# Hash logits in two packed products per half, and scores ahead of the transposes in every third step

## The chip, the cores and the metric

The kernel runs on one core of a Trainium2 chip. The metric is the device time of the whole program in microseconds. The engines are TensorE (PE in the rows; its weight loads are PEld), VectorE (DVE), ScalarE (ACT), GpSimd (POOL) and SyncE, whose queue (SPq) issues most transfers.

## What is computed

LSH attention over 16 heads (batch 2, 8 heads) of 768 tokens and 64 dimensions, all in float32, and then two dense layers with 1536 tokens:

```
q_bits = (q @ proj > 0); k_bits = (k @ proj > 0)         # proj: 64 x 6
mask   = (bucket(q_bits)[:, None] == bucket(k_bits)[None, :])
scores = where(mask, q @ k.T / sqrt(64), -1e9)
attn   = exp(scores - max); attn /= sum(attn) + 1e-9
x      = attn @ v, as 1536 x 512
x      = gelu_sigmoid(x @ w_in) @ w_out                   # 512 -> 2048 -> 512
out    = mish(x @ w_in2) @ w_out2
```

The products must keep float32 precision, so the kernel splits each operand into a high part that TensorE takes at full speed (fp32r) and a rest, and adds three products: high by high, high by rest, rest by high.

## The kernel before

**Stages.** The attention fills the first 225 us. It is one loop over 96 steps (`NSTEP`); a step is a tile of 128 queries of one head, six steps (`NT`) a head. The two dense layers follow; their weights are fetched, decoded and split during the last heads already (`wfetch`, `wgo`), and so are sums of blocks of the first layer's weights (`ssums`, `ssplit`) and factors of the attention's result (`x_ops`), which the dense layers need.

**Scores with the mask in them.** `qk` (L613) makes a step's scores with four products of 384 columns: `kh` and `qx` carry the high part of k against q and its rest, `kb` and `qb` carry the rest of k and, in rows 0 to 63, the hash bits. These bits add a large number to every pair whose buckets differ, and `clamp` (L625, VectorE) cuts the score at 1e9 while it takes the row's minimum. `expo` (L638, ScalarE) is the exponential with the row sum.

**Transposes and values.** Three steps are a group. `trp` (L676) transposes the exponentials of three steps, three 128 x 128 blocks into one PSUM bank, of which there are three (`ps_t`, "pt"; the logits and the row sums use the same three). ScalarE casts a bank to the high part (`pth`, L683), VectorE subtracts it (`trl`, `ptl`, L688), and `pv` (L700, L701) multiplies both with v (`vv`). The transposes lag `LAG` = 3 steps behind the scores, the products with v 4.

**A head's preparation.** `prep(n)` gives the parts of head n; `start_prep` places them by step (`at(step, f)`, run where `T` stands in the order), counted from `b0` = 6 (n - 2), two heads ahead of the head's use, so in the same row of six steps as the attention of head n - 2. `load_q` and `load_k` bring 64 and 128 rows. On GpSimd `s0` and `s1` (at b0 + 2) scale q into its high part `qk_m` (L473), scale again and subtract for the rest (L476, L477 into `qx`), round k (`kh`, L109), and subtract (L481). A DMA copies the q part to the other partitions of `qx` (L474). At b0 + 8 `s2` makes the **logits**: `logits` (L493) is called for both halves of 384 tokens, and multiplies `qk_m`, `kh` and `qx` with a projection padded to 128 columns (`pwt`), six products into one bank, rows 64 to 127 for the first half and 0 to 63 for the second. In the same step VectorE compares and scales all 128 rows at once (`s2m`, constants in `mc`), and at b0 + 9 `s5` sends the mask's rows to `qb` and `kb` with four DMAs of 32 rows. `s4` sends two rests, `s3` makes `vv`.

**Row sums and result.** `norm1` to `norm3` transpose the row sums of two heads (L657), write them to DRAM and broadcast them (`rb`); `x_out` (L725, L731, L732) multiplies the result by them on GpSimd, and `x_split` and `x_ops` (L109, L301, L309, L313) make the factors.

**Order.** Within a step the string `ORDER` sets what each engine's queue gets: A and B the transposes, a and b the residues, C the clamp, E the exponential, Q the next step's scores, T the work placed by `at`, P and R the products with v. Every engine takes its instructions in this program order. `SSP` and `WOF` are tables of steps for the weight sums and for the first weights:

```
ORDER = "ACaBbETQPR"
SSP = (-13, -11, -10, -9, -7, -6)
```

Of the kernel before, what the change touches and what calls it, by code (L numbers as in the profile page):

```python
# [30 lines left out]
def mask_consts():  # L31
    c = np.zeros((64, 2), np.float32)
    c[12:18, 0] = -3.0e38
    c[0:18, 1] = 1.0
    c[38:44, 0] = -3.0e38
    c[32:38, 1] = -2.0 * CBIG
    c[38:50, 1] = CBIG
    return np.concatenate([c, c])
# [3 lines left out]
def lsh_attention_moe_kernel(  # L42
# [9 lines left out]
    nc = tc.nc  # L52
    B, H, D, S = qt.shape
    NTOK, DM = out.shape
# [11 lines left out]
    SSP = (-13, -11, -10, -9, -7, -6)  # L66
    WOF = ((-1, -1, 11, 14, 18), (-1, 1, 11, 13, 17))
# [3 lines left out]
    POOLW = ()  # L71
    X0 = (1, 6)
# [150 lines left out]
    def wsplit(k, sub):  # L223
# [127 lines left out]
    def attention():  # L351
        with ExitStack() as es:
# [79 lines left out]
            def zero_rows():  # L432
                for t in (kb_tiles[1], qb_tiles[1]):
                    pcopy(t[32:64], zero[32:64])

# [8 lines left out]
            def pcol(j, o):  # L444
                w = pw[:, j, o : o + 2 * NB * (2 if o else 1)]
                return w.rearrange("p (a b) -> p a b", a=2)[:, :, 0:NB]

            def prep_w():
# [6 lines left out]
                nc.scalar.mul(pcol(0, 0), rnd(pr), -1.0)  # L455

            opnd = {}

            def prep(n):
# [12 lines left out]
                def s0():  # L472
                    nc.gpsimd.tensor_scalar(qk_m[0:D], qn[0:D], QSCALE, 1.0, ALU.mult, ALU.mult)  # L473
                    nc.sync.dma_start(rnd(qx[D:P]), rnd(qk_m[0:D]))  # L474
                    if n > 1:
                        nc.gpsimd.tensor_scalar(qn[0:D], qn[0:D], QSCALE, 1.0, ALU.mult, ALU.mult)  # L476
                        nc.gpsimd.tensor_sub(qx[0:D], qn[0:D], rnd(qk_m[0:D]))  # L477

                def s1():
                    pcopy(kh, kn)  # L480
# [20 lines left out]
                def s2():  # L501
                    pt = ps_t.tile([P, 512], F32, tag="pt", name="prep")
                    logits(pt, 0, 64, True, False)
                    logits(pt, 1, 0, False, True)
                    mk_box.append(pt)
                    if n > 1:
                        s2m()

                def s2m():
                    pt = mk_box.pop()  # L510
# [6 lines left out]
                def s4():  # L517
                    nc.sync.dma_start(rnd(qb[D:P]), rnd(qk_m[0:D]))
                    nc.sync.dma_start(rnd(kb[D:P]), rnd(qk_m[D:P]))

                def s5():
                    mk = mk_box.pop()
                    for f in range(2):
                        c = slice(f * HS, (f + 1) * HS)
                        rows = (qb, f * D), (kb, f * D + 32)
                        for t, r in rows[::-1] if f else rows:
                            nc.sync.dma_start(rnd(t[0:32, c]), mk[r : r + 32])
# [62 lines left out]
                return s0, s1, s2, s3, s4, s5  # L590
# [162 lines left out]
            ORDER = "ACaBbETQPR"  # L753
            NZ = 5
            NZL = 2
            PVLAG = LAG + 1
            todo = {}

# [7 lines left out]
            at(1, zero_rows)  # L766

# [3 lines left out]
            def start_prep(n):  # L771
                b0 = NT * (n - 2)
                s0, s1, s2, s3, s4, s5 = prep(n)
# [17 lines left out]
            for u in range(NHD // 2):  # L791
# [6 lines left out]
                at(zs + nz + (2 if u < NHD // 2 - 1 else 1), norm3, u)  # L798
# [22 lines left out]
            for i in range(NSTEP + PVLAG):  # L821
# [14 lines left out]
                for op in ORDER if i != 2 else ORDER.replace("TQ", "QT"):  # L836
# [402 lines left out]
def layouts(q, k, v, proj, moe_w_in, moe_w_out, moe2_w_in, moe2_w_out):  # L1239
# [3 lines left out]
    qt = q.transpose(0, 1, 3, 2)  # L1243
# [44 lines left out]
```

## Time and profile before

| | before |
|---|---|
| median of three runs | 730.86 us (730.52 to 731.77) |
| the profiled execution | 731.06 us, of which its span is 729.3 us |
| mean granted TensorE clock | 0.999 |
| TensorE busy | 723.5 us, 99% |
| VectorE busy | 616.3 us, 85% |
| ScalarE busy | 469.0 us, 64% |
| GpSimd busy | 185.4 us, 25% |

The span runs from the first to the last instruction of one profiled execution; 1.8 us lie around it. Busy shares are means over the whole span. GpSimd's work lies nearly all in the attention, the first 225 us, so its share of that stage is much higher than 25%.

### The profile page before, as it was taken

The page shows a single profiled execution, that of the slowest core. Times are in us where ns is not written, and L with a number is a line of the kernel's source. Part 1 is how long each engine was busy: PE and PEld are TensorE (multiplying, and loading weights), DVE is VectorE, ACT ScalarE, POOL GpSimd, SP SyncE. Part 2 cuts the span into 40 slices and gives each one's busy share as a digit, 9 for nine tenths or more (in the row PEclk, how much of TensorE's full clock was granted, in tenths as well). Part 3 has the DMA queues.
Part 4 walks back from the last instruction along what each step waited for, and adds up shares of the span by engine and source line. Part 5 has one row for each costly group of instructions (what it writes and reads, how often), then busy time and mean ns, then how long its engine had stood idle before and what let it go on. Part 6 is the DMA issues. An engine that isn't in the chain of part 4 may idle for free.

```text
span 729.3 us, 11137 instructions
## 1 busy us (share of the span) xinstructions
PE 723.5 (99%) x3856; PEld 631.5 (87%) x3856; DVE 616.3 (85%) x1134; ACT 469.0 (64%) x957; POOL 185.4 (25%) x187
## 2 busy tenths in 40 slices
PE   8999999999999999999999999999999999999998
PEld 6999999999998788888888888888888888888886
DVE  8888889989888959878878797998699899897864
ACT  7888888888898765536546465576635656455340
POOL 7968877889893000000000000000000000000000
PEclk9999999999999999999999999999999999999999
DMA  5745656666624221121211221301302121211004
GB/s 157 199 125 145 190 141 163 182 157 153 170 85 118 109 70 48 58 87 64 82 58 58 88 88 60 112 0 59 115 0 87 59 75 69 88 58 58 1 1 173
DMA packets 25992, 69.53 MB, mean 95 GB/s; under 512 B 4464, under 2 KB 6992, under 8 KB 25936
## 3 DMA queue, kind: packets, MB, share of 16 engines
q1 hardware_dynamic: 25632, 68.62, 31.7%
q8 instruction: 30, 0.49, 0.3%
q10 hardware_dynamic: 304, 0.20, 0.1%
q14 instruction: 26, 0.21, 0.1%
HBM read 49.09 MB, written 3.19 MB: 72 GB/s over the span
## 4 chain that ended last, share of the span: by engine, by line
PE 94%; DVE 2%; ACT 2%; DMA 0%; issue 0%; DVEq 0%
PE y L947 36%; PE X L1010 11%; PE s L613 9%; PE pt L676 9%; PE Y L1010 8%; PE W L1010 7%; PE u L701 4%; PE u L700 4%; PE h L346 4%; PE prep L493 2%; ACT p L638 1%; DMA qn<-in_qt_dram 0%; ACT pth L683 0%; DVE gl L907 0%; DVE Y L1031 0%
## 5 line engine op out<-in xcount | busy, mean ns | idle before, releaser
L688 DVE TENSOR_TENSOR ptl<-pt,pth 128x384 fp32r<-128x384 f32 x192 | 98.1, 553 | 22.4 <-ACT pth L683 20.2
L683 ACT CAST pth<-pt 128x384 fp32r<-128x384 f32 x192 | 82.8, 484 | 28.7 <-PE pt L676 28.7
L638 ACT ACTIVATE p<-p,mn 128x768 f32<-128x768 f32 x96 | 91.2, 950 | 1.7 <-DVE p L625 1.6
L625 DVE TENSOR_SCALAR_CACHE_REDUCE p<-s 128x768 f32<-128x768 f32 x96 | 90.6, 945 | 0.3 <-PE s L613 0.2
L961 DVE TENSOR_TENSOR xq<-xq,y 128x512 f32<-128x512 f32 (+1 forms) x113 | 75.6, 679 | 13.7 <-PE y L947 13.0
L676 PE MATMUL pt<-ident,p 128*128 128x128 f32 x576 | 81.1, 274 | 0.1
L947 PE MATMUL y<-wh,gh 128*128 128x512 f32 (+1 forms) x194 | 75.4, 389 | 0.0
L947 PE MATMUL y<-wl,gh 128*128 128x512 f32 (+1 forms) x194 | 75.4, 389 | 0.0
L947 PE MATMUL y<-wh,gl 128*128 128x512 f32 (+1 forms) x194 | 75.2, 387 | 0.0
L947 PE MATMUL y<-gh,wh 128*128 128x512 f32 x192 | 75.0, 391 | 0.0
L947 PE MATMUL y<-gh,wl 128*128 128x512 f32 x192 | 74.9, 390 | 0.0
L947 PE MATMUL y<-gl,wh 128*128 128x512 f32 x192 | 74.7, 389 | 0.0
L259 ACT CAST wh<-wb 128x512 fp32r<-128x512 f32 x64 | 39.4, 620 | 54.5 <-DVE wb L246 26.2
L676 PEld LDWEIGHTS pt<-ident,p 128*128 128x128 f32 x576 | 68.5, 140 | 6.6 <-ACT p L638 2.4
L700 PE MATMUL u<-pth,vv 128*128 128x384 f32 x192 | 64.7, 337 | 0.0
L701 PE MATMUL u<-ptl,vv 128*128 128x384 f32 x192 | 64.5, 336 | 0.0
L613 PE MATMUL s<-kh,qx 128*128 128x384 f32 x192 | 55.7, 370 | 0.2 <-DVE p L625 0.2
L613 PE MATMUL s<-kb,qb 128*128 128x384 f32 x192 | 49.3, 337 | 0.3 <-POOL qk_m L473 0.2
L261 DVE TENSOR_TENSOR wl<-wb,wh 128x512 fp32r<-128x512 f32 x62 | 42.3, 687 | 3.9 <-ACT wh L259 3.6
L961 DVE TENSOR_TENSOR yr<-yr,y 128x512 f32<-128x512 f32 x56 | 38.2, 684 | 7.8 <-PE y L947 6.9
L947 PEld LDWEIGHTS y<-wh,gl 128*128 128x128 f32 x194 | 36.4, 188 | 7.6
L947 PEld LDWEIGHTS y<-wh,gh 128*128 128x128 f32 x194 | 36.5, 188 | 7.3 <-DVE xq L961 0.4
(272 smaller groups left out, 1842.1 us busy)
## 6 DMA issues: line engine op xcount, KB each, us to landing
raw<-in_wt_dram SPq DMA_DIRECT2D x64, 512.0 KB, 3.6
kn<-in_kt_dram SPq DMA_DIRECT2D x15, 384.0 KB, 4.2
vn<-in_vt_dram SPq DMA_DIRECT2D x8, 384.0 KB, 5.3
ul<-uh SPq DMA_DIRECT2D x16, 192.0 KB
rb<-scr SPq DMA_DIRECT2D x16, 192.0 KB, 3.5
qn<-in_qt_dram SPq DMA_DIRECT2D x15, 192.0 KB, 3.4
qx<-qk_m SPq DMA_DIRECT2D x15, 192.0 KB, 3.9
qb<-qk_m SPq DMA_DIRECT2D x15, 192.0 KB, 5.6
```

The costliest lines, as they stand in the source:

```text
L261: sub(lo, wf, rnd(hi))
L613: nc.tensor.matmul(s[:, f, :HS], a[:, c], bb[:, f * HS : (f + 1) * HS], start=st, stop=not st,)
L625: nc.vector.tensor_scalar(sb, s[:, :, :HS], NEG, None, ALU.min, ALU.min, accum_out=mn)
L638: nc.scalar.activation(p, p, AF.Exp, bias=mn, scale=-1.0, accum_out=z_t[u][:, zc : zc + 1],)
L676: nc.tensor.transpose(ptile[:, j * P : (j + 1) * P], p_t[3 * g + j][:, t * P : (t + 1) * P], ident,)
L683: nc.scalar.copy(hi, ptile[:, :HS])
L688: nc.vector.tensor_sub(lo, ptile[:, :HS], rnd(hi))
L700: nc.tensor.matmul(ut[:, :HS], vv[:, t, :], hi, start=(t == 0), stop=False)
L701: nc.tensor.matmul(ut[:, :HS], vv[:, t, :], lo, start=False, stop=(t == NT - 1))
L947: nc.tensor.matmul(y, w[:, js] if m == 0 else x[:, js], x if m == 0 else w[:, i0:i1], start=(n == 0), stop=(n == 5),)
L961: nc.vector.tensor_add(acc, acc, y)
L1010: nc.tensor.matmul(bk[b], w[:, k], x, start=(first and i == 0), stop=(hook is not None and i == 2), skip_group_check=True,)
```

## The change

**Logits from the third head on (n > 1).** The host gives q twice, on 128 partitions, so `load_q` moves 384 KB. `s0` rounds k and q on all 128 partitions (`kh`, `qx`), and then subtracts to get the rests, in `qx[0:64]` and in `qk_m[64:128]`; the high part of k comes into `qk_m[0:64]` by a DMA (`s6`). With that, `qx` and `qk_m` each hold a high part and a rest, and each half of the tokens needs two products with a packed projection `px` (140 columns, made once by `prep_x` at step 4, with a clear on GpSimd, three copies there and two small DMAs): one for q and one for k, into one bank. The logits come a step earlier, at b0 + 7. Rows 64 to 127 of the bank hold what rows 0 to 63 are compared with: ScalarE negates them into `mk` in the logits' step, VectorE compares behind the next step's clamp (`mid`), and GpSimd multiplies 32 rows of `mk` by -2 CBIG behind that (for head 2 ScalarE does). `s5` sends 12 rows each instead of 32, at b0 + 8.

**Order.** In steps whose number is a multiple of three (but not 0) the next scores stand first, ahead of the transposes and of the clamp (`EARLY_Q`).

**Places.** The broadcasts of the row sums (`norm3`) of the first six pairs of heads come two steps later. The weight sums and their split stand at steps -11 to -6 instead of -13 to -6, two of the weight steps at +13 instead of +11, and the low bits of the weights 0 and 1 are made on ScalarE instead of VectorE.

The diff, cut to what the text speaks of:

```diff
-    SSP = (-13, -11, -10, -9, -7, -6)
-    WOF = ((-1, -1, 11, 14, 18), (-1, 1, 11, 13, 17))
+    SSP = (-11, -10, -9, -8, -7, -6)
+    WOF = ((-1, -1, 13, 14, 18), (-1, 1, 13, 14, 17))
...
+    MKA = (2,)
...
-        if k < NDVE:
+        if 1 < k < NDVE:
...
-                    nc.sync.dma_start(t[0:D], qt[b, h])
+                    nc.sync.dma_start(t, qt[b, h])
...
+            px = wo[0].tile([P, DM], F32R, tag="ol1", name="px")[:, 0:280]
+            px = px.rearrange("p (a b) -> p a b", a=2)
...
                 def s0():
+                    if n > 1:
+                        pcopy(kh, kn)
+                        nc.gpsimd.tensor_scalar(qx, qn, QSCALE, 1.0, ALU.mult, ALU.mult)
+                        nc.gpsimd.tensor_scalar(qn[0:D], qn[0:D], QSCALE, 1.0, ALU.mult, ALU.mult)
+                        nc.gpsimd.tensor_sub(qx[0:D], qn[0:D], rnd(qx[0:D]))
+                        return
...
+                    if n > 1:
+                        for f in range(2):
+                            for j, x in enumerate((qx, qk_m)):
+                                nc.tensor.matmul(
+                                    pt[:, :HS],
+                                    px[:, j, 12 - 12 * f : 140 - 12 * f],
+                                    x[:, f * HS : (f + 1) * HS],
+                                    start=(f + j == 0),
+                                    stop=(f + j == 2),
+                                )
+                        mk = hd.tile([P, HS], F32, tag="mk", name="mk", bufs=1)
+                        mk_box.append(mk)
+                        nc.scalar.mul(mk[0:64], pt[64:128, :HS], -1.0)
+                        return
...
+                        nc.vector.tensor_tensor(mk[0:64], pt[0:64, :HS], mk[0:64], ALU.is_gt)
+                        if n in MKA:
+                            nc.scalar.mul(mk[32:64], mk[32:64], -2.0 * CBIG)
+                        else:
+                            nc.gpsimd.tensor_scalar(
+                                mk[32:64], mk[32:64], -2.0 * CBIG, 1.0, ALU.mult, ALU.mult
+                            )
+                        return
...
+                def s6():
+                    nc.sync.dma_start(rnd(qk_m[0:D]), rnd(kh[0:D]))
...
+            EARLY_Q = "QACaBbETPR"
...
-                for f, early, late in ((s2, 8, 8), (s3, 11, 6), (s4, 6, 5), (s5, 9, 9)):
+                for f, early, late in ((s6, 5, 3), (s2, 8, 7), (s3, 11, 6), (s4, 6, 5), (s5, 9, 8)):
                     at(early if n == 2 else b0 + late, f)
+                mid.setdefault(9 if n == 2 else b0 + 8, []).append(s2m)
...
-                at(zs + nz + (2 if u < NHD // 2 - 1 else 1), norm3, u)
+                at(zs + nz + (4 if u < NHD // 2 - 2 else NHD // 2 - u), norm3, u)
...
-                for op in ORDER if i != 2 else ORDER.replace("TQ", "QT"):
+                for op in ORDER.replace("TQ", "QT") if i == 2 else ORDER if i % 3 or not i else EARLY_Q:
...
                         clamp(i)
+                        for f in mid.pop(i, ()):
+                            f()
```

How the queues change is shown at three places. In the rows, names follow the text above; lines are those of each kernel's own file, in which L676, L613, L700 and L701 have become L722, L659, L746 and L747.

TensorE at the logits of head 15, the last head, before: six products between the transposes and the next scores.

```order
L676 MATMUL pt<-ident,p 128x128 x6
L493 MATMUL prep<-qk_m,pwt 128x384
L493 MATMUL prep<-kh,pwt 128x384
L493 MATMUL prep<-qx,pwt 128x384
L493 MATMUL prep<-qk_m,pwt 128x384
L493 MATMUL prep<-kh,pwt 128x384
L493 MATMUL prep<-qx,pwt 128x384
L613 MATMUL s<-kh,qx 128x384 x2
L613 MATMUL s<-kb_141,qb_139 128x384 x2
```

After, the same place: four.

```order
L722 MATMUL pt<-ident,p 128x128 x6
L525 MATMUL prep<-qx,px 128x384
L525 MATMUL prep<-qk_m,px 128x384
L525 MATMUL prep<-qx,px 128x384
L525 MATMUL prep<-qk_m,px 128x384
L659 MATMUL s<-kh,qx 128x384 x2
L659 MATMUL s<-kb_141,qb_139 128x384 x2
```

The products with `kh` are gone, and `qx` and `qk_m` take turns against `px`.

TensorE over two steps behind the logits of head 15, before: the transposes (L676) come ahead of the scores (L613) in every step.

```order
L676 MATMUL pt<-ident,p 128x128 x6
L613 MATMUL s<-kh,qx 128x384 x2
L613 MATMUL s<-kb_141,qb_139 128x384 x2
L700 MATMUL u<-pth,vv 128x384
L701 MATMUL u<-ptl,vv 128x384
L700 MATMUL u<-pth,vv 128x384
L701 MATMUL u<-ptl,vv 128x384
L676 MATMUL pt<-ident,p 128x128 x6
L613 MATMUL s<-kh,qx 128x384 x2
L613 MATMUL s<-kb_141,qb_139 128x384 x2
```

After, the same two steps:

```order
L722 MATMUL pt<-ident,p 128x128 x6
L659 MATMUL s<-kh,qx 128x384 x2
L659 MATMUL s<-kb_141,qb_139 128x384 x2
L746 MATMUL u<-pth,vv 128x384
L747 MATMUL u<-ptl,vv 128x384
L746 MATMUL u<-pth,vv 128x384
L747 MATMUL u<-ptl,vv 128x384
L659 MATMUL s<-kh,qx 128x384 x2
L659 MATMUL s<-kb_141,qb_139 128x384 x2
L722 MATMUL pt<-ident,p 128x128 x6
L746 MATMUL u<-pth,vv 128x384
```

In the second of the steps the scores (L659) have moved ahead of the transposes (L722).

GpSimd near the end of the attention, before: from the first weight sum (`sf`, L277) to the fourth (L283), with the values of head 15 (`vv`), the row sums (`z`) and the factors of x between them.

```order
L277 TENSOR_TENSOR sf<-wb 128x256
L109 TENSOR_SCALAR vv<-vn 128x6x64
L582 TENSOR_TENSOR vv<-vn,vv 128x6x64
L650 TENSOR_SCALAR z<-z 128x12
L313 TENSOR_TENSOR xq<-xq 128x512 x2
L279 TENSOR_TENSOR sf<-wb 128x256
L109 TENSOR_SCALAR t2h<-xq 128x512
L301 TENSOR_TENSOR t2l<-xq,t2h 128x512
L281 TENSOR_TENSOR sf<-sf,wb 128x256
L315 TENSOR_TENSOR xq<-xq 128x512
L109 TENSOR_SCALAR b21h<-xq 128x512
L283 TENSOR_TENSOR sf<-wb,sf 128x256
```

After, the rows up to the fourth sum (now L286):

```order
L316 TENSOR_TENSOR xq<-xq 128x512 x2
L280 TENSOR_TENSOR sf<-wb 128x256
L547 TENSOR_SCALAR mk<-mk 32x384
L112 TENSOR_SCALAR t2h<-xq 128x512
L304 TENSOR_TENSOR t2l<-xq,t2h 128x512
L282 TENSOR_TENSOR sf<-wb 128x256
L318 TENSOR_TENSOR xq<-xq 128x512
L112 TENSOR_SCALAR b21h<-xq 128x512
L284 TENSOR_TENSOR sf<-sf,wb 128x256
L304 TENSOR_TENSOR b21l<-xq,b21h 128x512
L112 TENSOR_SCALAR t3h<-xq 128x512
L286 TENSOR_TENSOR sf<-wb,sf 128x256
```

The first sum stands behind the products of `xq`, the factor of the mask of head 15 (`mk`, L547) behind that, and `b21l` and `t3h`, which stood behind the fourth sum, now stand ahead of it.

On ScalarE the cast of the four sums (`sh`, L291, now L294) keeps its place, behind the copy `zt` (L663) and ahead of the casts of step 90.

## Rows read from the trace of the kernel before

**Rows 1.** The page's first part: busy us, share of the span, instructions.
```profile
PE 723.5 (99%) x3856; PEld 631.5 (87%) x3856; DVE 616.3 (85%) x1134; ACT 469.0 (64%) x957; POOL 185.4 (25%) x187
```

**Rows 2.** The page's fourth part: shares of the chain that ended last.
```profile
PE 94%; DVE 2%; ACT 2%; DMA 0%; issue 0%; DVEq 0%
```

**Rows 3.** Timeline of TensorE, 98.6 to 108.2: start us, us, what, xcount [idle before <-releaser].
```profile
102.27 0.82 PE L676 MATMUL pt<-ident,p 128*128 128x128 f32 x6
102.84 0.59 PE L613 MATMUL s<-kh,qx 128*128 128x384 f32 x2
...
105.15 0.34 PE L493 MATMUL prep<-kh,pwt 128*128 128x384 f32 x1
...
106.02 0.51 PE L613 MATMUL s<-kh,qx 128*128 128x384 f32 x2
...
107.41 0.81 PE L676 MATMUL pt<-ident,p 128*128 128x128 f32 x6
```

**Rows 4.** Waits, 18 to 222: waiter <- releaser: us in total, times, longest us.
```profile
PEld pt L676 <- ACT p L638: 2.2, 9, 0.3
```

**Rows 5.** Timeline of TensorE, 107 to 115.
```profile
113.55 1.03 PE L676 MATMUL pt<-ident,p 128*128 128x128 f32 x6
```

**Rows 6.** Timeline of ScalarE, 107.5 to 114.
```profile
107.93 0.86 ACT L683 CAST pth<-pt 128x384 fp32r<-128x384 f32 x2 [1.24 <-PE pt L676]
...
112.08 0.86 ACT L683 CAST pth<-pt 128x384 fp32r<-128x384 f32 x2 [0.26 <-PE pt L676]
112.83 0.95 ACT L638 ACTIVATE p<-p,mn 128x768 f32<-128x768 f32 x1
```

**Rows 7.** Groups of GpSimd, 0 to 225: busy, mean ns | idle before, releaser.
```profile
L109 POOL TENSOR_SCALAR vv<-vn 128x384 fp32r<-128x384 f32 x16 | 8.3, 516 | 3.0 <-issue 2.5 <-PE u L701 0.2
...
L109 POOL TENSOR_SCALAR qb<-qx 64x384 fp32r<-64x384 f32 x2 | 2.1, 1055 | 0.1
```

**Rows 8.** Timeline of GpSimd, 166 to 210.
```profile
168.47 0.83 POOL L473 TENSOR_SCALAR qk_m<-qn 64x768 fp32r<-64x768 f32 x1
...
182.97 0.83 POOL L473 TENSOR_SCALAR qk_m<-qn 64x768 fp32r<-64x768 f32 x1 [1.03 <-DMA qn<-in_qt_dram]
...
192.78 0.73 POOL L731 TENSOR_TENSOR xq<-ul,rb 128x256 f32<-128x256 f32 x1 [1.49 <-DMA rb<-scr]
...
195.60 0.74 POOL L277 TENSOR_TENSOR sf<-wb 128x256 f32<-128x256 f32 x1 [0.84 <-DVE wb L243]
...
205.97 0.75 POOL L283 TENSOR_TENSOR sf<-wb,sf 128x256 f32<-128x256 f32 x1
206.67 1.29 POOL L301 TENSOR_TENSOR b21l<-xq,b21h 128x512 fp32r<-128x512 f32 x1
...
208.50 1.31 POOL L261 TENSOR_TENSOR wl<-wb,wh 128x512 fp32r<-128x512 f32 x1
```

**Rows 9.** Timeline of all engines, 168.5 to 171.5.
```profile
168.57 0.59 PE L613 MATMUL s<-kh,qx 128*128 128x384 f32 x2
...
169.07 1.02 DVE L688 TENSOR_TENSOR ptl<-pt,pth 128x384 fp32r<-128x384 f32 x2 [0.34 <-ACT pth L683]
...
170.01 0.95 DVE L625 TENSOR_SCALAR_CACHE_REDUCE p<-s 128x768 f32<-128x768 f32 x1
...
170.62 0.59 PE L613 MATMUL s<-kh,qx 128*128 128x384 f32 x2
```

**Rows 10.** Timeline of ScalarE, 203.4 to 217.
```profile
208.80 1.04 ACT L291 CAST sh<-sf 128x1024 fp32r<-128x1024 f32 x1
209.75 0.83 ACT L683 CAST pth<-pt 128x384 fp32r<-128x384 f32 x2
...
214.21 0.94 ACT L638 ACTIVATE p<-p,mn 128x768 f32<-128x768 f32 x1
```

**Rows 11.** Stretch at the end: us, busy (x) by engine, PEclk, DMA share, GB/s.
```profile
726.30:729.30 3.00, 0.00 (x0) 0.00 (x0) 0.23 (x1) 0.00 (x0) 0.00 (x0) 0.77 0.43 151
```

**Rows 12.** Timeline of TensorE, 0 to 5.2.
```profile
0.77 3.57 PE L423 MATMUL warm<-const-bfloat16-1.0 128*128 128x512 bf16 x8 [0.77 <-PEq L1268]
```

More of the change, by code (lines that the diff above doesn't have):

```diff
@@ L33, in mask_consts @@
     c[12:18, 0] = -3.0e38
[L34 to L37, printed above, removed]
+    c[0:12, 1] = 1.0
+    c[12:18, 1] = -0.5
+    c[32:38, 0] = -3.0e38
+    c[32:38, 1] = CBIG
+    c[38:50, 1] = -2.0 * CBIG
     return np.concatenate([c, c])
@@ L53, in lsh_attention_moe_kernel @@
     B, H, D, S = qt.shape
+    D //= 2
     NTOK, DM = out.shape
@@ L434, in zero_rows @@
                     pcopy(t[32:64], zero[32:64])
+                nc.gpsimd.memset(rnd(px), 0.0)
             wzero = pp.tile([P, 7, 64], F32, tag="p", name="wzero")
@@ L444, in pcol @@
             def pcol(j, o):
-                w = pw[:, j, o : o + 2 * NB * (2 if o else 1)]
-                return w.rearrange("p (a b) -> p a b", a=2)[:, :, 0:NB]
+                o += NB if o else 0
+                return pw[:, j, o : o + 2 * NB].rearrange("p (a b) -> p a b", a=2)
             def prep_w():
@@ L455, in prep_w, with prep_x @@
                 nc.scalar.mul(pcol(0, 0), rnd(pr), -1.0)
+            px = wo[0].tile([P, DM], F32R, tag="ol1", name="px")[:, 0:280]
+            px = px.rearrange("p (a b) -> p a b", a=2)
+            def prep_x():
+                o = 32 + NB
+                q, k, ql, kl = (slice(x, x + 2 * NB) for x in (12, 44, 76, 108))
+                pcopy(px[:, 0, q], rnd(pw[:, 0, 0 : 2 * NB]))
+                pcopy(px[0:D, 1, k], rnd(pw[0:D, 1, o : o + 2 * NB]))
+                pcopy(px[D:P, 1, k], rnd(pw[D:P, 2, o : o + 2 * NB]))
+                nc.sync.dma_start(rnd(px[D:P, 0, ql]), rnd(pw[0:D, 2, 0 : 2 * NB]))
+                nc.sync.dma_start(rnd(px[0:D, 1, kl]), rnd(pw[D:P, 1, o : o + 2 * NB]))
             opnd = {}
@@ L502, in s2, with s2m @@
                     pt = ps_t.tile([P, 512], F32, tag="pt", name="prep")
+                    mk_box.append(pt)
+                    if n > 1:
[12 more added lines that the diff above has]
+                        return
                     logits(pt, 0, 64, True, False)
                     logits(pt, 1, 0, False, True)
-                    mk_box.append(pt)
+                def s2m():
                     if n > 1:
-                        s2m()
-                def s2m():
+                        pt, mk = mk_box
+                        del mk_box[0]
+                        nc.vector.tensor_tensor(mk[0:64], pt[0:64, :HS], mk[0:64], ALU.is_gt)
[6 more added lines that the diff above has]
+                        return
                     pt = mk_box.pop()
@@ L524, in s5 @@
                         c = slice(f * HS, (f + 1) * HS)
-                        rows = (qb, f * D), (kb, f * D + 32)
-                        for t, r in rows[::-1] if f else rows:
-                            nc.sync.dma_start(rnd(t[0:32, c]), mk[r : r + 32])
+                        rows = (qb, f * D, 0, 32), (kb, f * D + 32, 0, 32)
+                        if n > 1:
+                            rows = (qb, f * 12, 0, 12), (kb, f * 12 + 32, 6, 12)
+                        for t, r, a, w in rows[::-1] if f else rows:
+                            nc.sync.dma_start(rnd(t[a : a + w, c]), mk[r : r + w])
                 def first(q1, k1):
@@ L757, in attention @@
             todo = {}
+            mid = {}
             def at(step, f, *args):
@@ L766, in attention @@
             at(1, zero_rows)
+            at(4, prep_x)
             for f, st in zip(second[3:7], (2, 7, 1, 3)):
```

12 lines of the change are left out of this document (4 added, 8 removed).

## The prediction

> **What bounds the kernel now.** I read the page first: TensorE is busy for 99% of the span, GpSimd for 25% [rows 1], and the chain that ended last is TensorE for 94% [rows 2]. GpSimd's 25% is a mean over two stages: nearly all its work lies in the attention, the first 225 us, and the change lies there too.
>
> Then the timeline of TensorE in the attention. A step (one tile of 128 queries of one head, 96 in all) is four score products, six transposes and four products with v. Products of 384 columns start 0.174 us apart: from 105.15 to 106.02 five starts pass. Six transposes show as 0.82 us, of which 0.57 is pitch (102.27 to 102.84) [rows 3]. So a step is 8 x 0.174 + 6 x 0.109 = 2.05 us, and six logits products add 1.04 us once per head: 13.3 us, of the 13.53 that a head takes. There is hardly a hole.
>
> The view of waits names the rest: weight loads of the transposes waited 2.2 us for ScalarE's exponentials, 9 times, 0.3 at most [rows 4]. They stand at the first transposes of a group of three steps, whose third block is the exponential of the step just before: 1.03 us where 0.82 is normal [rows 3, 5].
>
> **What the change takes away.** Heads 2 to 15 need four logits products, not six: 14 x 2 x 0.174 = **4.9 us** off an engine without holes. Their operands need the same five GpSimd operations in another order, and one copy between partitions in place of another.
>
> Every third step the next scores stand ahead of the transposes, which gives the exponential 4 x 0.174 = 0.70 us more. The waits were 0.3 us at most, so they go: **2.2 us**.
>
> The price is that a group's casts, residues and exponentials come 0.70 us later, and the loop from one group's transposes to the next's must still close. ScalarE takes from 107.93 to 112.83 + 0.95 = 113.78, 5.85 us, for three steps, with a hole of 0.26 in it; the first cast comes 0.52 us after its transposes (107.41), and the third block is needed 0.22 us after the first [rows 3, 6]. 0.52 + 5.85 - 0.26 - 0.22 = 5.9 us against TensorE's 3 x 2.05 = 6.15: it closes with some 0.25 us to spare. In the half of a head that holds the logits, TensorE gives 0.70 us and ScalarE gets one negation more, 0.43 us (half of a pair of casts [rows 6]). It closes there too. I cost it at nothing; rival D is the case in which it doesn't close.
>
> With both terms and nothing new the profiled run would go from 731.06 to 724.0 us, the median (0.2 lower) to 723.8.
>
> **What the change adds: GpSimd waits for VectorE once per head.** The mask's factor is a new GpSimd instruction, 32 x 384, behind VectorE's comparison, and GpSimd takes its instructions in order. Its price isn't in the trace: 128 x 384 of the same operation took 0.52 us, 64 x 384 in the first microseconds 1.06 [rows 7]. I take 0.5, from the steady stage, and keep 1.0 as the other end; it is an added instruction, so it can't gain.
>
> Its price is small; its place is not. Before, GpSimd ran ahead of TensorE as soon as loads had landed: the preparation of head 14 began at 168.47, before step 74 began at 170.62 [rows 8, 9]. Now the whole preparation of head n stands behind the factor of head n-1, so behind the third step of its window. For most heads this costs nothing: the work of a window stays just under its 13.0 us. For head 14 it doesn't, since factors of the first matrix layer are queued there: 182.97 - 1.03 - 168.47 = 13.5 us [rows 8], with the new factor 14.0, and head 15's is longer. I follow GpSimd from that gate:
>
> - Step 74 began at 170.62. Eleven heads' logits come ahead of it (11 x 0.348 = 3.83 less), head 13's four products now stand ahead of it (0.70 more), and of the waits some 1.7 us: 165.8.
> - VectorE's clamp starts 1.44 us after a step begins (168.57 to 170.01), takes 0.95, the comparison 0.5 (residues of 384 columns: two in 1.02 [rows 9]): 168.7. With the factor 169.2, where before the same preparation began at 168.47: 0.7 later.
> - From there to the end of the fourth sum of weights (205.97 + 0.75 = 206.72) GpSimd had work without a break but for three waits, 1.03 + 1.49 + 0.84 = 3.36 us. These vanish, as the queue is late. Added are two more factors (1.0) and two operations that now stand ahead of the fourth sum, because the sums are placed two steps later (206.67 to 208.50, 1.83) [rows 8]. 206.72 + 0.7 - 3.36 + 1.0 + 1.83 = **206.9 us**: the same absolute time as before, while TensorE should be 6.6 us ahead.
>
> ScalarE's cast of these sums (sh) stands where it stood, ahead of the casts of step 90. Before, it began at 208.80, 2.1 us after the sums were there, and the casts at 209.75 [rows 10]. After, ScalarE would reach it near 202.2 and **wait some 4.7 us**; the casts of step 90 start at 206.9 + 0.95 = 207.85. TensorE can't run past this: there are three PSUM banks for transposes, so the second transposes of step 91 wait for a residue of step 90 (about 1 us behind the cast, an estimate from the pair of residues [rows 9]): 208.8. From there to the third block of step 93 it has its own work, 0.33 + 0.70 + 0.69 + 0.65 + 0.70 + 0.69 + 0.70 + 0.22 = 4.7 us: 213.5. Before, that block had to wait for the exponential, 214.21 + 0.94 = 215.15 [rows 10], and the scores of step 94 (0.70) came behind it; now they are done. So the stage ends 1.7 + 0.7 = **2.4 us** earlier. The rest is carried along, since the matrix layers are TensorE without holes; GpSimd's last factors end at about the absolute time they did, well ahead of their first readers.
>
> 731.06 - 2.4 = 728.7; on the scale of the median **728.5 us**. Of 7.1 us some 4.7 would stay in ScalarE's wait for GpSimd.
>
> Four edits I cost at nothing. The row broadcasts, two steps later, go out behind the mask's transfers, and GpSimd reaches their product some 8 us behind the factor. The doubled q load is issued four steps ahead of its use. The high-bit work of weights 0 and 1 that moves from VectorE to ScalarE falls in a half with logits, or ahead of one. At the start about 1.3 us of new GpSimd work (the packed projection) comes ahead of head 2, whose logits have about that to spare. Without its cover each would be under 1 us, once.
>
> **Rivals.**
> A. *GpSimd is in time*, by instructions shorter than I sum or by another order of waits: the 4.7 us vanish and both terms stay. For it: my lateness is a difference of large numbers. Against: these durations hardly vary. 723.8 us.
>
> B. *The hole lets TensorE's clock fall.* The hole at step 91 is 3 to 4.7 us. From 726.3 to 729.3 no product ran and the mean granted clock is 0.77, so it left the upper level (2.4 GHz) for the lower one (1.2) some 1.6 us in [rows 11]. At the start eight products of 512 columns took 3.57 us, before the upper level [rows 12]. One such stretch at half speed loses 1.75 us: 728.5 + 1.75 = 730.2 us. The Trainium skill, "TensorE: Matmul & The Clock Gate", section "What's actually happening", says that the throttled state is the default and activity releases it. The trace agrees at both ends of the run; by that rule the hole would cost this stretch too.
>
> C. *The waits for exponentials stay*, as the added negations eat the 0.70 us. Step 74 then begins 1.7 us later, and with it GpSimd's gate: 730.2 us. For it: only 0.25 us of room. Against: the half with the logits has more.
>
> D. *The loop of a group doesn't close*, the slower side. If scores in front push the loop from transposes to transposes past 6.15 us, each half of a head takes the excess. It decides at 6.76 us (half of 13.53): above it heads are longer than before. At 7.0 us, 1.1 more than I read, a head takes 14.0 and 14 heads 6.6 us more than before: 737 us.
>
> **How the numbers follow.** Forecast 45% (727.3 to 729.7: a factor of 0.4 to 1.0 us three times, and the gate), A 20% (723.0 to 725.0), B 14%, C 12%, D 9%. The range takes in A from 723.2 and reaches over B and C: 723.2 to 730.9; the forecast's own is 727.3 to 729.7. A measurement here can tell 0.2%, 1.5 us: faster is under 729.4. That holds A, most of the forecast and a little of B and C: 0.66. Same is the rest of the forecast, B and C: 0.25. Slower is D: 0.09.
>
> **What would show it.** The logits: 56 products behind head 1, where 84 were. The transposes of every third step at 0.82 us. GpSimd without a break from about 169 on, the factor of head 15 some 4 us behind its comparison. ScalarE idle ahead of the cast of sh for 4 to 5 us, released by GpSimd, and one hole of TensorE of 3 to 5 us between 201 and 209. If that wait is under 1 us, my account of GpSimd's queue is wrong and the time is A's. If the granted clock shows 0.5 there, B holds.

## The result, and the profile after

The changed kernel takes 739.1 us (738.12 to 739.70), 1.0109 times the kernel before (95% interval 1.0094 to 1.0124): **1.1% slower**, where I forecast 728.5 us. The profiled execution has a span of 736.3 us, 7.0 more than before. The page's busy times (share of the span, instructions), and the shares of the chain that ended last, against [rows 1, 2]:

```profile
PE 725.2 (98%) x3828; PEld 627.6 (85%) x3828; DVE 611.7 (83%) x1132; ACT 474.8 (64%) x974; POOL 193.1 (26%) x204
...
PE 88%; POOL 3%; DVE 2%; ACT 2%; DMA 2%; SPq 1%; issue 1%; POOLq 0%; DVEq 0%; ACTq 0%
```

TensorE has the 28 instructions less that were promised, and GpSimd now holds 3% of the chain. Where the 7 us arise is read from VectorE's clamps of steps 18, 72 and 95 (start us, us), first of before, then of after:

```profile
45.87 0.95 DVE L625 TENSOR_SCALAR_CACHE_REDUCE p<-s 128x768 f32<-128x768 f32 x1
167.77 0.95 DVE L625 TENSOR_SCALAR_CACHE_REDUCE p<-s 128x768 f32<-128x768 f32 x1
219.21 0.95 DVE L625 TENSOR_SCALAR_CACHE_REDUCE p<-s 128x768 f32<-128x768 f32 x1
```

```profile
46.84 0.95 DVE L671 TENSOR_SCALAR_CACHE_REDUCE p<-s 128x768 f32<-128x768 f32 x1
168.54 0.95 DVE L671 TENSOR_SCALAR_CACHE_REDUCE p<-s 128x768 f32<-128x768 f32 x1
226.38 0.95 DVE L671 TENSOR_SCALAR_CACHE_REDUCE p<-s 128x768 f32<-128x768 f32 x1
```

The start is 1.0 us longer, with two waits of TensorE that were not there before:

```profile
15.08 0.55 PE L722 MATMUL pt<-ident,p 128*128 128x128 f32 x3 [0.51 <-DVE ptl L734]
...
30.34 0.41 PE L746 MATMUL u<-pth,vv 128*128 128x384 f32 x1 [0.71 <-ACT uh L758]
```

The nine heads from step 18 to 72 take 121.70 us, not 121.90: the gain that I put at 0.5 us a head is 0.02. The last 23 steps take 57.84, not 51.44: 6.4 us more.

**The heads.** The waits for exponentials of [rows 4] are gone from the view of waits, and others stand there (total us, times, longest):

```profile
PEld prep L525 <- issue: 2.2, 10, 0.2
PEld u L746 <- ACT uh L758: 1.9, 12, 0.2
...
PE s L659 <- DMA kb<-mk: 0.9, 2, 0.6
```

The first is that of the logits. TensorE at one of them (to be read against [rows 3]), and VectorE's residues there:

```profile
101.36 0.82 PE L722 MATMUL pt<-ident,p 128*128 128x128 f32 x6
101.93 0.42 PE L746 MATMUL u<-pth,vv 128*128 128x384 f32 x1
...
102.71 0.85 PE L722 MATMUL pt<-ident,p 128*128 128x128 f32 x6
103.56 0.41 PE L525 MATMUL prep<-qx,px 128*128 128x384 f32 x1
103.81 0.34 PE L525 MATMUL prep<-qk_m,px 128*128 128x384 f32 x1
```

```profile
102.40 1.02 DVE L734 TENSOR_TENSOR ptl<-pt,pth 128x384 fp32r<-128x384 f32 x2 [0.66 <-ACT pth L729]
```

From the transposes to the second logits product TensorE takes 1.10 us; six transposes and one product need 0.83. With the scores moved away, only four products stand between the transposes of two steps, and the logits behind them need the bank whose residue ends at 102.40 + 1.02 = 103.42.

**The end of the attention.** GpSimd's factors and fourth sum, ScalarE's cast of the sums, TensorE, and the stretch behind its hole (as rows 11: busy by engine, then the granted clock):

```profile
175.18 0.50 POOL L547 TENSOR_SCALAR mk<-mk 32x384 f32<-32x384 f32 x1 [1.16 <-PE s L659]
...
213.49 0.72 POOL L286 TENSOR_TENSOR sf<-wb,sf 128x256 f32<-128x256 f32 x1
```

```profile
214.25 1.04 ACT L294 CAST sh<-sf 128x1024 fp32r<-128x1024 f32 x1 [4.87 <-POOL sf L286]
```

```profile
208.65 0.42 PE L659 MATMUL s<-kb,qb 128*128 128x384 f32 x1 [0.64 <-DMA kb<-mk]
209.33 0.44 PE L659 MATMUL s<-kb,qb 128*128 128x384 f32 x1 [0.26 <-DMA kb<-mk]
...
216.31 0.90 PE L722 MATMUL pt<-ident,p 128*128 128x128 f32 x3 [3.47 <-DVE ptl L734]
...
219.58 0.63 PE L722 MATMUL pt<-ident,p 128*128 128x128 f32 x4
```

```profile
217.30:219.60 2.30, 2.30 (x9) 2.20 (x9) 2.14 (x6) 1.73 (x5) 2.26 (x2) 0.50 0.31 96
```

The sums are done at 214.21, ScalarE waited 4.87 us for them, and TensorE stood for 3.47 us. Behind that the granted clock is 0.50, the lower level: from 216.31 to 219.58 three transposes and eight products take 3.27 us, not 3 x 0.109 + 8 x 0.174 = 1.72: another 1.55 us. The mask of head 15 came late too: its scores start 0.8 and 0.5 us behind their pitch (208.65 and 209.33). 3.47 + 1.55 + 1.3 = 6.3 us of the 6.4. The 1.3 us are part of the sum, but no price of their own: the hole ends when the sums are there, so without the late mask it would by these rows be that much longer.

### The profile page after: what moved, and what is told of

Read it like the earlier page. It is cut to its first block, busy times and chain, and to the rows that moved or that the text cites. A ratio compares the mean times of both kernels' runs of the same rounds, so it can differ in the third digit from the quotient of the medians.

```text
span 736.3 us, 11214 instructions
## 1 busy us (share of the span) xinstructions
PE 725.2 (98%) x3828; PEld 627.6 (85%) x3828; DVE 611.7 (83%) x1132; ACT 474.8 (64%) x974; POOL 193.1 (26%) x204
## 4 chain that ended last, share of the span: by engine, by line
PE 88%; POOL 3%; DVE 2%; ACT 2%; DMA 2%; SPq 1%; issue 1%; POOLq 0%; DVEq 0%; ACTq 0%
PE y L999 36%; PE X L1062 11%; PE Y L1062 7%; PE W L1062 7%; PE s L659 7%; PE pt L722 7%; PE h L349 4%; PE u L746 4%; PE u L747 3%; PE prep L525 2%; DMA kn<-in_kt_dram 1%; DMA kb<-qk_m 1%; ACT pth L729 1%; DMA qn<-in_qt_dram 0%; ACT p L684 0%
## 5 line engine op out<-in xcount | busy, mean ns | idle before, releaser
L722 PE MATMUL pt<-ident,p 128*128 128x128 f32 x576 | 80.4, 275 | 4.1 <-DVE ptl L734 4.0
L722 PEld LDWEIGHTS pt<-ident,p 128*128 128x128 f32 x576 | 68.4, 141 | 10.0 <-DVE ptl L734 5.0
L746 PE MATMUL u<-pth,vv 128*128 128x384 f32 x192 | 69.2, 361 | 0.7 <-ACT uh L758 0.7
L747 PE MATMUL u<-ptl,vv 128*128 128x384 f32 x192 | 64.9, 338 | 0.0
L659 PE MATMUL s<-kh,qx 128*128 128x384 f32 x192 | 53.5, 359 | 0.2 <-DVE p L671 0.2
L659 PE MATMUL s<-kb,qb 128*128 128x384 f32 x192 | 50.0, 340 | 1.2 <-DMA kb<-mk 0.9
```

The source lines that it names most:

```text
L659: nc.tensor.matmul(s[:, f, :HS], a[:, c], bb[:, f * HS : (f + 1) * HS], start=st, stop=not st,)
L722: nc.tensor.transpose(ptile[:, j * P : (j + 1) * P], p_t[3 * g + j][:, t * P : (t + 1) * P], ident,)
L746: nc.tensor.matmul(ut[:, :HS], vv[:, t, :], hi, start=(t == 0), stop=False)
L747: nc.tensor.matmul(ut[:, :HS], vv[:, t, :], lo, start=False, stop=(t == NT - 1))
```

## The experiments

A head's length below is a fourth of the time from head 3's first logits product to head 7's. It is 13.53 us before and 13.49 after.

| run | median us | ratio to before (95%) | head us | ScalarE's wait for the sums |
|---|---|---|---|---|
| changed kernel | 739.1 | 1.0109 (1.0094-1.0124) | 13.49 | 4.9 |
| e1_no_early_q | 738.8 | 1.0104 (1.0089-1.0119) | 13.44 | 4.6 |
| e2_before_early_q | 735.9 | 1.0065 (1.0050-1.0080) | 13.85 | - |
| e3_logits_behind_scores | 736.8 | 1.0079 (1.0064-1.0095) | 13.25 | 5.4 |
| e4_split_later | 736.1 | 1.0063 (1.0046-1.0080) | 13.51 | - |
| e5_no_negation | 737.6 | 1.0077 (1.0062-1.0092) | 13.44 | 4.8 |
| e7_all_waits | 733.9 | 1.0029 (1.0018-1.0041) | 13.27 | - |
| e8_all_waits_old_order | 734.7 | 1.0043 (1.0028-1.0058) | 13.46 | - |
| e9_logits_alone_step8 | 738.5 | 1.0101 (1.0085-1.0118) | 13.23 | - |
| e10_logits_alone_step7 | 734.6 | 1.0046 (1.0029-1.0063) | 13.43 | - |
| e11_factor_on_dve | 735.8 | 1.0059 (1.0041-1.0078) | 13.50 | 4.2 |
| e12_q_first_factor_dve | 736.0 | 1.0067 (1.0052-1.0082) | 13.65 | 0.8 |
| e13_q_first | 739.6 | 1.0116 (1.0101-1.0131) | 13.49 | 4.8 |
| e14_logits_step8_free | 754.3 | 1.0336 (1.0284-1.0387) | 14.1 | 3.5 |
| e15_all_parts_free | 734.6 | 1.0044 (1.0029-1.0059) | 13.63 | 0.2 |
| e16_waits_away_again | 732.0 | 1.0009 (0.9999-1.0018) | 13.25 | - |

### Which part spoils the heads: e1, e2, e5

e1 is the changed kernel with `for op in ORDER if i != 2 else ORDER.replace("TQ", "QT")` in every step.

> The changed kernel with the old order in every step: scores never stand ahead of the transposes; all else as changed. Theory BANK (the four logits products save 0.35 us a head, but with the scores moved away the transposes of two steps stand 0.7 us closer and the logits wait 0.25 us for one of the three banks, the first product with v 0.1 us for the copy of u): the wait of 0.25 us a head is gone, the waits for exponentials are back (some 0.15 us every second head), a head takes 13.2 us, not 13.5, the start loses 0.7 us of wait less, and the hole of 4 to 5 us before step 93 stays, since GpSimd's gate moves with TensorE: about 735.5 us (734.5 to 737). Theory LOOP (the group's loop through ScalarE, with one more negation, is too long whatever the order): heads stay at 13.5 us, 738 to 740 us.

e2 is the kernel before with this order alone:

```diff
-                for op in ORDER if i != 2 else ORDER.replace("TQ", "QT"):
+                for op in ORDER.replace("TQ", "QT") if i == 2 else ORDER if i % 3 or not i else "QACaBbETPR":
```

> The kernel before with the scores ahead of the transposes in every third step, and nothing else. Its logits stand one step later than in the changed kernel, behind a step in its usual order, so by BANK they do not wait for a bank: the 2.2 us of waits for exponentials go, some 0.1 us a head for the copy of u and 0.7 us at the first group come: 730 us (729 to 731.5), no logits wait. By LOOP (scores in front lengthen the loop of a group by themselves) heads get longer than 13.53 us: 733 us or more.

Both expectations of my theory missed, and the numbers of LOOP came out in both; what speaks against LOOP is e3 below, where heads take 13.25 us with the same instructions. Without the early scores the time is the same; early scores alone make every head of the old kernel 0.32 us longer. The waits of e1, then of e2, from 18 to 222 us:

```profile
PEld pt L722 <- ACT p L684: 5.1, 21, 0.4
```

```profile
PEld u L700 <- ACT uh L712: 3.9, 25, 0.2
```

In e1 the waits for exponentials are not 2.2 us but 5.1, 21 times and not 9. In e2 they are gone, but the first product of each group of values waits for ScalarE's copy of `u`, and the logits for a bank (in e2's trace 0.14 us at 107.18, where the six transposes from 106.47 need 0.57). So the early scores take one wait away and make two.

e5 takes ScalarE's negation out of e1:

```diff
-                        nc.scalar.mul(mk[0:64], pt[64:128, :HS], -1.0)
...
-                        nc.vector.tensor_tensor(mk[0:64], pt[0:64, :HS], mk[0:64], ALU.is_gt)
+                        nc.vector.tensor_scalar(mk[0:64], pt[0:64, :HS], 0.0, 1.0, ALU.is_gt, ALU.mult)
```

> As e1 (old order in every step), and ScalarE's negation of half of the logits' rows is left out: VectorE compares the other half with zero, so part of the hash's precision is left out. In e1 transposes waited 0.34 us a head for exponentials, before 0.14. Theory NEGATION (0.49 us more on ScalarE a head makes the exponentials late): the waits fall back to 0.14 us a head, 13 x 0.2 = 2.6 us less than e1, about 736 us. Theory SHORT (TensorE's 0.35 us less per head alone brings the transposes to ScalarE too early): the waits stay at 0.3 us or more, 738 to 739 us.

```profile
PEld pt L721 <- ACT p L683: 5.2, 21, 0.5
```

The waits stay, and so do the heads of 13.44 us: the extra work of ScalarE is not their cause. The time of 737.6 us lies between the two forecasts; the 1.2 us under e1 come at the end of the attention, not in the heads.

### Where the logits stand: e3, e9, e10

e3 moves the changed kernel's logits behind the next scores, in their own step:

```diff
-                for op in ORDER.replace("TQ", "QT") if i == 2 else ORDER if i % 3 or not i else EARLY_Q:
+                for op in ORDER.replace("TQ", "QT") if i == 2 or i % NT == 1 and i > 1 else ORDER if i % 3 or not i else EARLY_Q:
```

> The changed kernel, but in the logits' step the logits stand behind the next scores instead of ahead of them (0.7 us later); the same instructions on all engines. BANK: between the transposes and the logits TensorE has 0.7 us of scores, the wait of 0.25 us a head is gone, 13 x 0.25 = 3.2 us less up to step 74, and the hole moves with GpSimd's gate: about 736 us (735 to 737). LOOP: the wait appears at another product and heads stay at 13.5 us: 738.5 to 740 us.

```profile
101.83 0.85 PE L722 MATMUL pt<-ident,p 128*128 128x128 f32 x6
102.43 0.59 PE L659 MATMUL s<-kh,qx 128*128 128x384 f32 x2
...
103.21 0.34 PE L525 MATMUL prep<-qx,px 128*128 128x384 f32 x1
```

The logits wait for nothing, no new wait stands in their place, and a head takes 13.25 us. The bank was the wait, and the time, 736.8 us, is BANK's; with the same instructions on every engine 0.24 us a head come back.

e10 has the four logits products without the rest: old order, tables, low bits and broadcasts, and the factor on VectorE. e9 is the same with the logits at b0 + 8, where the kernel before has them:

```diff
-                for f, early, late in ((s6, 5, 3), (s2, 8, 7), (s3, 11, 6), (s4, 6, 5), (s5, 9, 8)):
+                for f, early, late in ((s6, 5, 3), (s2, 8, 8), (s3, 11, 6), (s4, 6, 5), (s5, 9, 9)):
...
-                mid.setdefault(9 if n == 2 else b0 + 8, []).append(s2m)
+                mid.setdefault(9 if n == 2 else b0 + 9, []).append(s2m)
```

> As the run before, and all places as in the kernel before: old order in every step, tables SSP and WOF, low bits and broadcasts where they were. What is left of the change is the logits in four products, at b0 + 7, and the factor on VectorE. Theory PLACE (before, the logits stood between the transposes of a group's third step and the first of the next, and gave the exponential there 1.04 us; one step earlier they don't, and the transposes wait 0.15 us at both group starts of a head): 0.35 us saved, 0.2 to 0.26 given back, 13 x 0.1 = 1.3 us: 729.6 us (728.8 to 730.6). If the waits are ScalarE's or VectorE's throughput: the same.

> As e10, with logits, comparison and the mask's transfers one step later, the logits at b0 + 8 as in the kernel before. PLACE: the wait for exponentials goes back to 0.14 us a head, a head takes 13.2 us: 730.8 - 14 x 0.35 = 726 us (725.5 to 728). Theory THROUGHPUT (ScalarE and VectorE need 13.45 us a head whatever the place): no faster than e10, 729 us or more.

The heads are as PLACE has them, 13.43 and 13.23 us; both times are missed. The waits for exponentials, 18 to 228, of e10 and then of e9:

```profile
PEld pt L719 <- ACT p L681: 5.5, 22, 0.6
```

```profile
PEld pt L719 <- ACT p L681: 1.9, 9, 0.4
```

At b0 + 8 four products stand between the transposes of a group's third step and the next group's first, and give the exponential of that step 0.70 us; at b0 + 7 they stand elsewhere, and both group starts of a head wait. That is what the change lost with its step earlier: at the old step, 0.30 of the 0.35 us of two products less are there. The step is not free to take back: e9's mask comes too late. SyncE, then TensorE:

```profile
109.25 1.11 SPq L712 DMA_DIRECT2D rb<-scr  x2
110.45 0.79 SPq L570 DMA_DIRECT2D qb<-mk  x1
```

```profile
113.73 0.92 PE L656 MATMUL s<-kb,qb 128*128 128x384 f32 x2 [2.31 <-DMA kb<-mk]
```

The mask's transfers stood behind the broadcasts `rb`, for which SyncE had waited 6.4 us:

```profile
SPq L712 <- DMA scr<-zt: 6.4, 1, 6.4
```

Three heads lost 1.8 to 3.4 us so (from a step's first score to its first product with v, 2.6 to 4.2 us where 0.8 is normal). It shows what the later broadcasts of the change are good for.

### GpSimd and the end: e4, e11, e12, e13, e14

e4 moves the split of the sums, and nothing else: `SSP = (-11, -10, -9, -8, -3, -2)`.

> The changed kernel with the cast and the rest of the four weight sums (sh, sl) four steps later, where GpSimd's sums are done; first read 30 us later. If ScalarE's wait of 4.9 us for the fourth sum makes TensorE's hole of 3.6 us and the lower clock behind it (some 1.6 us), both go: 739.1 - 5 = 734 us (733 to 735), no granted clock of 0.5 left. If the hole is made by the transposes' own loop or by the late mask of head 15, it stays: 738 us or more.

The wait of ScalarE, the hole and the low clock are gone, and so are 0.46% of the time (3.4 us). That it is not 5 is due to two new waits: the cast now stands ahead of a copy of `u`, and later a product waits for VectorE:

```profile
222.41 0.41 PE L746 MATMUL u<-pth,vv 128*128 128x384 f32 x1 [0.88 <-ACT uh L758]
242.11 0.50 PE L999 MATMUL y<-gl,wh 128*128 128x512 f32 x1 [0.69 <-DVE gl L959]
```

So the hole was ScalarE's wait for the sums. Why are they late? e11 puts the factor on VectorE; e12 also prepares q ahead of k (`pcopy(kh, kn)` from `s0` to the head of `s1`); e13 does only the latter.

```diff
-                            nc.gpsimd.tensor_scalar(
+                        nc.vector.tensor_scalar(
```

> The changed kernel with the factor of the mask on VectorE, right behind its comparison, for all heads; GpSimd has no instruction left that waits for TensorE's logits. Theory GATE (GpSimd, held at each head's factor, is 7 us late with the fourth weight sum and with head 15's mask): the hole of 3.6 us before step 93, the lower clock behind it and the wait for kb go, head 2's 0.9 us too; heads stay at 13.5 us: 739.1 - 5 - 1.3 - 0.9 = 732 us (731 to 733.5). Theory VOLUME (GpSimd is late because it has more to do, the sums being placed later): the hole stays, 737 us or more.

> As e11 (factor on VectorE), and GpSimd prepares q ahead of k, as the kernel before did. In e11 GpSimd still stood at 176.80 for the load of k, 3.61 us. In the changed kernel k is rounded first, k is loaded behind q, and q's load is twice as long, so the first operation needs both loads; before, q alone was needed and k 3.6 us later. Theory LOAD (the load of k is a second gate, as late as the factor): with both gates gone GpSimd is 4 us earlier, the hole goes, 732 us (731 to 733.5). Theory VOLUME: the hole stays, 735 us or more.

> The changed kernel with q ahead of k on GpSimd, and nothing else: the factor stays on GpSimd. LOAD with GATE (two gates of about the same time, the factor of head 13 at 175.2 and the load of k at 176): the factor still holds GpSimd, the hole stays at 3 us or more, 737 to 739 us. If the load alone was the cause: as e12.

The start of head 14's preparation and TensorE's hole, in e11, in e12, in e13:

```profile
176.80 0.83 POOL L112 TENSOR_SCALAR kh<-kn 128x768 fp32r<-128x768 f32 x1 [3.61 <-DMA kn<-in_kt_dram]
...
216.20 0.90 PE L719 MATMUL pt<-ident,p 128*128 128x128 f32 x3 [4.24 <-DVE ptl L731]
```

```profile
175.13 0.83 POOL L490 TENSOR_SCALAR qx<-qn 128x768 fp32r<-128x768 f32 x1 [1.05 <-DMA qn<-in_qt_dram]
...
214.98 0.55 PE L719 MATMUL pt<-ident,p 128*128 128x128 f32 x3 [0.78 <-DVE ptl L731]
```

```profile
176.31 0.50 POOL L547 TENSOR_SCALAR mk<-mk 32x384 f32<-32x384 f32 x1 [1.18 <-PE s L659]
...
217.40 0.68 PE L722 MATMUL pt<-ident,p 128*128 128x128 f32 x3 [3.46 <-DVE ptl L734]
```

Before, this preparation began at 168.47 [rows 8], in the changed kernel at 175.76. Of these 7.3 us the wait at this one factor is 1.16; GpSimd's work ahead of it ends at 174.02 only, for it is late from earlier heads already (head 13's preparation began at 161.78, before at 155.82). GpSimd in the changed kernel, then in e12:

```profile
173.82 0.20 POOL L696 TENSOR_SCALAR z<-z 128x12 f32<-128x12 f32 x1
```

```profile
170.22 0.74 POOL L774 TENSOR_TENSOR xq<-ul,rb 128x256 f32<-128x256 f32 x1 [2.39 <-DMA rb<-scr]
```

Four things can hold GpSimd: the factor, the load of k (now needed first), the load of q (twice as large), and the broadcasts of the row sums, which the change has two steps later. Each stands in for the other: with the factor gone k's load holds this start, with k second q's load does, for 1.05 us; and in e12 GpSimd waits six times for the broadcasts, 15.3 us in all, where the kernel before waits 1.75 us and the changed kernel shows none. In e12 the hole shrinks by 3.5 us, but only some 1.2 us of that is GpSimd's (its fourth sum ends at 212.86, in e11 at 214.10); TensorE itself comes later there, by waits for VectorE.

e11 and e12 miss both of their forecasts, at 735.8 and 736.0 us; e13 takes 739.6, with the hole as LOAD with GATE has it. The profile of e11 is of its slowest run, 738.95 us at a mean granted clock of 0.995; its other five took 733.5 to 736.2 us at 0.998 or 0.999, and what hole they have is not shown. So GATE as the single cause is refuted by that one profile and not by the times. The cause stays a sum, whose parts no run separates: these gates, then the sums behind more work.

e14 is e9 with the broadcasts behind the mask, q ahead of k, and the low bits on ScalarE:

> As e9 (old order, logits alone, at b0 + 8, factor on VectorE), where heads took 13.2 us until three heads waited 2.5 to 2.9 us for the mask's transfers, which stood in SyncE's queue behind the broadcasts of row sums waiting for their write; now the broadcasts stand behind the mask's transfers, q is prepared ahead of k, and the low bits of weights 0 and 1 are on ScalarE. If these are the whole of e9's loss: 14 heads at 0.35 us less, 731 - 4.5 = 727 us (726 to 729). If VectorE or ScalarE can't give heads of 13.2 us once weights are decoded: 731 us or more.

It is the worst of all, for a reason that I had not in view. VectorE, then GpSimd in e14:

```profile
112.53 0.54 DVE L543 TENSOR_TENSOR mk<-prep,mk 64x384 f32<-64x384 f32 x1
113.11 1.91 DVE L544 TENSOR_SCALAR mk<-mk 32x384 f32<-32x384 f32 x1
115.05 1.02 DVE L731 TENSOR_TENSOR ptl<-pt,pth 128x384 fp32r<-128x384 f32 x2
```

```profile
112.98 1.83 POOL L492 TENSOR_TENSOR qx<-qn,qx 64x768 fp32r<-64x768 f32 x1
```

The factor on VectorE takes 0.35 us where nothing disturbs it and 1.91 here, until GpSimd's subtraction ends (114.81); residues and transposes come later by it. What share of e14's 23 us this is was not measured: TensorE also waits for the mask's transfers there (5.4 us in all), and the hole of 3.3 us is back. All runs with the factor there (e9 to e12, e14, e15) carry this cost, so their times don't speak on the change itself; I use their head lengths only as far as no such wait is among them.

### All waits away: e7, e8, e15, e16

e7 takes away what the traces had named up to then (head 2's factor, not shown, moves behind the exponential); e8 is e7 in the old order.

```diff
+                for op in ORDER.replace("TQ", "QT") if i == 2 or i % NT == 1 and i > 1 else EARLY_Q if i % 3 == 0 and i > 3 else ORDER:
...
+    SSP = (-9, -9, -8, -8, -2, -1)
+    XOP = ((4, 1.22), (4, 0.56), (1, 0.41))
```

> The changed kernel with every wait that the traces name taken away: logits behind the next scores (as e3), scores in front only from step 6 on (the first group waited 0.67 us for a bank), head 2's factor on ScalarE behind the exponential and not ahead of it (0.88 us), the factors of x two steps later so that the factor of head 15's mask is not queued behind them (1.3 us of wait for kb), the four weight sums behind that factor, and their split five steps later, not ahead of a copy of u. If these waits are the whole of the loss, it is theirs less: 739.1 - 2.3 (measured by e3) - 0.7 - 0.9 - 1.3 - 5 = 729 us (727.5 to 730.5), faster than before by 0.2%. If the loss is a property of the loop, the waits reappear elsewhere and the time stays over 732 us.

> As e7, with the old order in every step, so that the scores never stand in front. If scores in front are worth something once the logits are out of their way, this is slower than e7 by the waits for exponentials less the waits for the copy of u: 13 x (0.42 - 0.21) = 2.7 us, about 731.5 us. If they are worth nothing, the same as e7 within 0.7 us.

e7 is not faster than before, against its forecast, but has heads of 13.27 us and no hole; e8 has 13.46. So in the heads of the table scores in front are worth 0.2 us once the logits are out of their way. Over the whole attention that is not left: from head 1's first logits product to the clamp of step 95 e7 takes 206.07 us (12.60 to 218.67) and e8 206.25 (12.11 to 218.36), and e8 is 0.85 us slower in the end, not 2.7. Early scores cost at the start what they give later. At step 93 e7 is 0.8 us ahead of the kernel before, and loses it behind, where my later places make TensorE wait:

```profile
221.68 0.66 PE L724 MATMUL pt<-ident,p 128*128 128x128 f32 x4 [0.82 <-ACT p L686]
228.68 0.27 PE L705 MATMUL prep<-ident,z 128*12 128x128 f32 x1 [0.89 <-DVE z L701]
```

> All parts of the change with the waits that the runs named taken away: as e12, logits behind the next scores (as e3), scores in front from step 6 on, and the steps of the weight sums as in the kernel before. Heads of 13.2 us (e3), no hole, no wait at the start: 731 - 13 x 0.3 + 0.5 = 727.5 us (726 to 729.5), faster than before. If a property of the loop sets the time: 731 us or more.

e15 takes the first two sums of weights before their low bits are set; its work is the same. It misses by VectorE's waits above.

e16 has e7's order, the changed kernel's places but for the split (`SSP = (-11, -10, -9, -8, 1, 2)`), and `MKA = (2, 14, 15)` behind the exponential.

> As e7, but nothing of the last stage is moved later except the split of the sums (to steps 97 and 98, where ScalarE has no exponentials left): factors of x and the sums stand where the changed kernel has them, and the factors of the masks of heads 14 and 15 are on ScalarE behind the exponential, so that GpSimd isn't held there. In e7 TensorE was 1.0 us ahead of the kernel before at step 93, and lost 3.8 us behind it to work placed later. If that is so: 731.5 - 1.0 = 730.5 us (729.5 to 732), about the kernel before. If ScalarE's two factors make a wait of their own, or the mask of head 15 is late again: 732 us or more.

732.0 us, 1.0009 times the kernel before (0.9999 to 1.0018): no difference. All of the loss is gone and 0.9 us of gain is there at step 95, but a product of the first matrix layer then waits for VectorE:

```profile
237.40 0.50 PE L1003 MATMUL y<-gl,wh 128*128 128x512 f32 x1 [1.38 <-DVE gl L963]
```

No version here beats the kernel before.

## Why the prediction was wrong

- **"4.9 us off an engine without holes"** is the step that failed. TensorE was 99% busy, but its head length was not the sum of its products alone: the transposes of a group waited for the exponential of the step before, and those six logits products, standing between, hid this wait in one of a head's two groups. I read the 2.2 us of waits as all there was. With four products a step earlier they become 5.1 us (e1). Of 0.35 us a head 0.09 is left; with four products at the old step (e9) it is 0.30, so what uncovers the wait is the step earlier more than the two products less.
- **"Scores in front: the waits go, 2.2 us"**: they go, but I followed the loop through ScalarE's exponentials only. I didn't follow the three banks (0.25 us a head) nor the one bank of `u` (0.1 us). Alone the early scores cost 0.32 us a head (e2). Together with the logits the two terms gave 0.04 us a head, not 0.5.
- **Rival D** had the right sign and a related mechanism, but a loop above 6.76 us is not what happened: heads did not get longer (13.49 us), they failed to get shorter. I gave the slower side 9%.
- **GpSimd's queue** was right in itself. From the start of head 13's factor to the end of the fourth sum I forecast 38.2 us, it took 39.0; the factor began at 175.18, not 168.7, since TensorE had not gained. Forecast and measured: ScalarE's wait 4.7 and 4.87 us, TensorE's hole 3 to 4.7 and 3.47, the factor 0.5 and 0.50. But I set this price against a gain that didn't exist. And I took the factor for the gate; it is one of four.
- **Rival B**, the lower clock behind the hole, held: 0.50, and 1.55 us where I had 1.75. I made it a rival to the forecast; it is a part of it.
- **The four edits at nothing**: the q load and the later broadcasts were not free (they hold GpSimd in e12; in the changed kernel the factor covers them). The 1.0 us at the start come with two waits that I had not listed, 0.51 us for a bank (15.08, the first group behind early scores) and 0.71 us for the copy of `u` (30.34). The first is gone in e7, where early scores begin later. The second takes ScalarE's factor for head 2, 0.53 us at 27.74 ahead of that copy, and the early scores together: it is gone in e11, which has this factor on VectorE, and in e1, in the old order; behind the exponential (e7) the factor still leaves 0.60 us.
- Two readings were loose, and nothing hangs on them: 0.57 us for six transposes is the time to the next product's start, and the 6 x 0.109 of the sum holds 0.08 us more, by which the first products behind them come later; and the fourth sum is placed one step later (-9 to -8), not two.

What stays open: how much of GpSimd's lateness is the factor, how much the doubled load, how much the later broadcasts and the order of SyncE's queue; no run has the single load or the earlier broadcasts with the changed kernel's other parts.

## What to carry to other kernels

An engine that is busy for 99% can still be paced by a chain through others: before counting a removed product as time, ask which wait it was hiding, and move it or shorten it only with that wait in view. When one queue's order changes, follow every resource that hands back to it (each PSUM bank, each copy that frees one), not only the chain that the edit is meant for. A loss that shows at one wait may have several gates at the same time, so that taking one away moves nothing.

## What I had not expected of the hardware

The same VectorE instruction, a factor on 32 x 384 in SBUF, took 0.35 to 1.98 us in e9, e11, e12 and e14 (fourteen in each), the longest beside GpSimd's subtractions of 1.83 us; on GpSimd it took 0.50 to 0.51 every time. The Trainium skill, "SBUF — State Buffer", section "SBUF: two separate sides", says that VectorE and GpSimd share a pair of ports that one instruction holds to its end. The trace agrees: the 1.91 us above end 0.2 us after GpSimd's instruction, and so do eleven more of the fourteen in e14 (0.21 to 0.23 us). The residues, which read one operand in PSUM, kept their 1.02 us a pair beside such work: in the kernel before the pair that starts at 171.14 lies wholly inside a subtraction (170.31, 1.84 us).
